# Causal attention and two feed-forward layers: odd heads' score halves swapped from the 13th pair on, and both decay products of those pairs on VectorE

## The chip, the cores and the metric

The kernel runs on one core of a Trainium2 chip. The metric is the device time of one execution in microseconds. TensorE (PE) multiplies matrices into PSUM, VectorE (DVE), ScalarE (ACT) and GpSimd (POOL) work element by element, and SyncE (SP) issues every DMA of this kernel, one after the other. Each engine runs its own list of instructions in order and waits for the others by semaphores.

## The reference, cut to what matters

```python
# attention: batch 4, heads 8, sequence 768, head_dim 48
for t in range(S):
    cur = einsum('bhd,bhe->bhde', u * k[t], v[t])
    y[t] = einsum('bhd,bhde->bhe', r[t], state + cur)
    state = w[t][..., None] * state + einsum('bhd,bhe->bhde', k[t], v[t])
# then, on (3072, 384) tokens:
xn = x / sqrt(mean(x * x) + 1e-6) * rms_g
x = (silu(xn @ w_gate) * (xn @ w_val)) @ w_out          # d_ff 1536
y = (s * relu(x @ w_in) ** 2 + b) @ w_out               # d_ff 2048
```

## The kernel before

The sequence is cut into 6 chunks of 128 tokens. A chunk of one batch row is a pair, numbered jb = 0 to 23 (chunk jb // 4, batch row jb % 4); the 13th pair is jb = 12. A pair's attention is worked as follows.

- DMAs bring w, then r and k together, then r and k by token (`n`), then v.
- VectorE scans the decays into `E` (line 357) and, backwards, into `bk` (line 364). Both are the tile `eb`, of which the later pairs have one copy, so the scan of the next pair waits until all readers of the last are done. r is multiplied by `E` and k by `bk`, in place in the tile `in` (`tt`, recorded at line 316); from jb = 12 on either engine, VectorE or GpSimd, may take each product, as the planner decides.
- `scores` (line 404): PE multiplies k by r. Two heads share a tile, one in partitions 0 to 47 and one in 64 to 111 (p = 0, 1, which write two PSUM banks); h = 0 to 3 counts the tiles. Only tokens of k not later than those of r count, so k's tokens 0 to 63 (c0 = 0) meet 128 columns of r, and tokens 64 to 127 (c0 = 64) only the last 64. The k half sits in columns c0 to c0 + 63 of PE's array and its result in the same partitions of PSUM. So each matmul uses a quarter of the array.
- ScalarE copies each score bank to a tile `a`, and GpSimd clears what lies above the diagonal (`affine_select`, line 426).
- `sums`: `state` (line 445) multiplies r by the state, line 454 multiplies `a` by v into the same banks, and `news` (line 463) multiplies the transposed k (`raw`, brought by four `kt` DMAs from `kd`) by v for the next state. VectorE adds `av` into `ys` and the news into `st`; the result is normalised and, from jb = 12 on, transposed through DRAM (`turn_x`: `pat`, then `xt` DMAs).

Meanwhile PE works through the first feed-forward layer, chunk after chunk, in steps f: `mm_in` for gate and for value (line 646, nine matmuls of 128x512 each, in banks 0 and 1), ScalarE's silu and VectorE's product (`sg`, which reads the value's bank), ScalarE's `hh` and VectorE's `hl`, and three `mm_out` of three matmuls each (lines 629 to 631) into banks 2, 3 and 4. After the last f of a chunk these banks are copied out (`o`, line 681 on ScalarE, 683 on VectorE) before the next chunk's first `mm_out` writes them.

Nothing of the order is written by hand. `op` hands each operation with a due time, a cost for each engine that may take it and what it reads and writes to `Plan`; `Plan.issue` plays the plan through with these costs and emits the instructions in the order in which that play starts them. A table, `FIRST_OPS`, replaces due times by operation number up to number 921; jb = 12 begins at operation 964. So a new operation or cost shifts the order of all engines after it.

Of the kernel before, what the change touches and what calls it, by code (L numbers as in the profile page):

```python
# [17 lines left out]
ALU = mybir.AluOpType  # L18
# [4 lines left out]
B, H, S, D = 4, 8, 768, 48  # L23
C = 128
NC = S // C
HP = H // 2
DM = H * D
# [20 lines left out]
W_TINY, W_HUGE = 1.125 * 2.0 ** -15, 1.875 * 2.0 ** 16 - 2.0 ** -7  # L48
FA, HALF = 6, (4, 6)
ATT = 30.0, 6.0, 0.0, 18.0, 20.0, 20.0, 20.0, 0.0  # L50
TD, LATE = 3, 60
ORDER = -200, -190, -170, -160, -180, -150
FIRST_OPS = {
# [170 lines left out]
def body(ctx: ExitStack, tc: tile.TileContext, rkw, nat, w1, w2, cst, out):  # L224
    nc = tc.nc
# [5 lines left out]
    def tiles(n, name, shape, dt=F32):  # L231
        return [sb.tile(shape, dt, name=f"{name}{i}") for i in range(n)]
# [15 lines left out]
    OT = tiles(2, "o", [128, NB])  # L248
    IN = tiles(2, "in", [128, RKW])
    VT = tiles(2, "v", [128, H, D])  # L250
    NT, = tiles(1, "n", [128, 2, H, D])
    EB = [[t] for t in tiles(2, "eb", [RW, HP, WL])]
    KT = tiles(1, "kt", [128, HP, RW])
# [48 lines left out]
    def op(when, engines, fn, reads=(), writes=(), port=True):  # L302
        if planned[0]:
            reads, writes = [alias.get(k, k) for k in reads], [alias.get(k, k) for k in writes]
            plan.add(when, engines, fn, reads, writes, port)
        else:
            fn(next(iter(engines)))

    def dma(when, dst, src, nbytes, reads=(), writes=(), land=0.0):
        op(when, {"sp": max(0.47, nbytes / 350e3 + 0.06) + 0.5 * (when == -300)}, lambda e: nc.sync.dma_start(  # L310
            out=dst, in_=src), reads, writes, land)
# [23 lines left out]
    def attention(jb, t):  # L335
        q, b = jb % 2, jb % B
        AVK = [("av", q, h0) for h0 in range(0, H, 2)]
        ke, re, ne = (DVE, DVE, DVE) if jb < EARLY else (BOTH, BOTH, BOTH)
        last = jb >= NJ - B
        a, v, g, z = IN[q][:RW], VT[q], RG[q], q if jb < NZ else 0  # L340
        n = [RK[z][:, i * DM:(i + 1) * DM].rearrange("p (h d) -> p h d", h=H) for i in range(2)]
        ET, BT, kt, xg = EB[0][z], EB[1][z], KT[z], XG[z]
        ek, bk, nk, tk, xk = ("E", z), ("bk", z), ("n", z), [("kt", z)], ("xg", z)
        turned = jb >= TURNED
        rk = RK[z][:RW, 0:HP * C].rearrange("p (h t) -> p h t", h=HP)
        r = a[:, OR:OK].rearrange("p (h t) -> p h t", h=HP)
        k = a[:, OK:].rearrange("p (h t) -> p h t", h=HP)
# [5 lines left out]
        if jb >= NU:  # L353
            dma(tl[2], RK[z], nat[jb, :, DM:], 128 * 2 * DM * 4, (), [nk])
        dma(tl[3], v.rearrange("p h d -> p (h d)"), nat[jb, :, 0:DM], 128 * DM * 4, (), [("v", q)])

        op(t, {"dve": 1.15}, lambda e: nc.vector.tensor_tensor_scan(
            ET.rearrange("p h t -> p (h t)"), a[:, 0:HP * WL], ones.rearrange("p h t -> p (h t)"), 0.0,
# [39 lines left out]
        def scores(e):  # L398
            for h in range(HP):
                for c0 in (0, 64) if jb >= B else (0,):  # L400
                    cols = slice(c0, c0 + 64 if jb >= B else C)
                    for p in range(2):
                        rows = slice(64 * p, 64 * p + D)
                        nc.tensor.matmul(sc[p][cols, h, c0:], k[rows, h, cols], r[rows, h, c0:],  # L404
                                         start=True, stop=True, skip_group_check=True)
            if kp is not None:
                for h in range(HP):
                    nc.tensor.transpose(kp[:, h, :], k[:, h, :], ident[:RW, :RW])  # L408
# [12 lines left out]
        for p in range(2):  # L421
            if jb < NM:
                tt(t, DVE, HP * C, AT[A[p]], sc[p], mask, ALU.mult, [("ps", i2[p]), "m"], [("a", A[p])])
                continue
            cp(t, HP * C, AT[A[p]], sc[p], [("ps", i2[p])], [("a", A[p])])
            op(t, {"pool": 0.60}, lambda e, s=A[p]: nc.gpsimd.affine_select(  # L426
                out=AT[s], in_=AT[s], compare_op=ALU.is_gt, fill=0.0, base=0, pattern=[[0, HP], [1, C]],
                channel_multiplier=-1), (), [("a", A[p])])
        if kp is not None:
            cp(t, HP * RW, kt, kp, [("ps", i)], tk)  # L430
        if jb < NU:
# [16 lines left out]
        def sums(e):  # L448
            if jb >= B:
                state(e)  # L450
            for j in range(H):
                h, p = divmod(j, 2)
                for c0 in (0, 64):
                    nc.tensor.matmul(Y[p][c0:c0 + 64, j, :], AT[A[p]][:, h, c0:c0 + 64], v[:, j, :],  # L454
                                     start=jb < B and j == 0, stop=j >= H - 2, skip_group_check=True)
            if U is not None and jb >= B:
                news(e)
# [19 lines left out]
        if jb < B:  # L477
            op(t, {"pe": 1.0}, sums, reads + [("v", q)], [("ps", i)])
            op(t, {"pe": 0.7}, more, AVK + ["cs"], [("ps", i)])
            op(t, {"pe": 0.6}, news, [("v", q)] + tk, [("ps", iu)])  # L480
            ys, yk = PS[i][:, 0:DM], ("ps", i)
        else:
            op(t, {"pe": 1.5 + 0.6 * (not last)}, sums,
               reads + [("r", q), ("v", q), ("st", b)] + tk * (not last),
               [("ps", i) for i in iy] + ([] if last else [("ps", iu)]))
            ys, yk = YS[q], ("ys", q)
            for p in range(2):
                y2, a2, s2 = [x.rearrange("p (h j d) -> p h j d", h=HP, j=2)[:, :, p] for x in (
                    PS[iy[p]][:, 0:DM], AV[q].rearrange("p h d -> p (h d)"), ys)]
                tt(t, DVE, HP * D, s2, y2, a2, ALU.add, [("ps", iy[p])] + AVK, [yk])  # L490
# [403 lines left out]
    for c in range(NC):  # L894
        t2 = T1 + c * d2
        x = c % 2
# [139 lines left out]
```

## Time and profile before

| | |
|---|---|
| time, median of 3 runs | 967.43 us (966.9 to 967.6) |
| the profiled execution | 967.64 us, of which its span is 965.9 us |
| PE busy | 952.9 us, 99% of the span |
| DVE, ACT, POOL busy | 635.2, 378.8 and 162.6 us |
| the chain that ended last | PE 91%, DVE 5%, DMA 2%, ACT 1% |

Busy time of PE is the time in which any of its pipelined matmuls was under way, so it says that PE was never without work, and not that it was at its peak. The profiled execution is one run; its time lies 0.2 us above the median.

### The profile page before, as it was taken

Reading aid. Unit: us, or ns where it says so; the run is one execution under the profiler, and the core shown is the slowest. Engines: PE = TensorE matmul, PEld = TensorE weight load, DVE = VectorE, ACT = ScalarE, POOL = GpSimd, SP = SyncE. Lnnn points to the kernel's source line nnn. Section 1 sums busy time; section 2 is a strip of 40 time slices with the busy share of each in tenths; the row PEclk is TensorE's granted clock in tenths of the full one; section 3 lists DMA queues with packets and bytes.
Section 4 is the critical chain, followed back from the end, with each engine's and each line's share of the span. In section 5 each row is a group of like instructions: output and inputs, shape, how many; then the busy total and the mean of one; then the engine's idle time right before and its main releaser. Section 6 shows DMA issues by size and latency. Waiting matters only on the chain.

```text
span 965.9 us, 16522 instructions
## 1 busy us (share of the span) xinstructions
PE 952.9 (99%) x6585; PEld 788.7 (82%) x6589; DVE 635.2 (66%) x1051; ACT 378.8 (39%) x782; POOL 162.6 (17%) x211
## 2 busy tenths in 40 slices
PE   9999999999999999999999999999999999999996
PEld 5898998888888887888888878888888888888885
DVE  8999898547445445532588799987777874433332
ACT  4756545534323332332343353343433433433333
POOL 1212211255433323110025440000000000000000
PEclk9999999999999999999999999999999999999998
DMA  8655554245434443222466465553354530000001
GB/s 259 196 169 158 173 158 140 83 112 149 101 84 118 122 93 95 69 69 61 122 225 206 150 212 178 158 194 113 114 182 132 178 117 1 33 0 1 34 1 36
DMA packets 74422, 115.79 MB, mean 120 GB/s; under 512 B 28384, under 2 KB 48096, under 8 KB 74336
## 3 DMA queue, kind: packets, MB, share of 16 engines
q1 hardware_dynamic: 74336, 114.65, 39.6%
q8 instruction: 53, 0.87, 0.4%
q14 instruction: 33, 0.27, 0.1%
HBM read 99.16 MB, written 15.47 MB: 119 GB/s over the span
## 4 chain that ended last, share of the span: by engine, by line
PE 91%; DVE 5%; DMA 2%; ACT 1%; issue 1%; SPq 0%; POOL 0%; DVEq 0%
PE b L646 48%; PE b L629 12%; PE b L630 11%; PE b L631 11%; PE b L454 2%; PE b L404 2%; PE b L445 1%; DMA raw<-in_w 1%; DMA in<-in_rkw 1%; DVE pat L605 1%; DVE pat L603 1%; PE b L408 0%; PE b L822 0%; PE b L469 0%; DVE pat L599 0%
## 5 line engine op out<-in xcount | busy, mean ns | idle before, releaser
L646 PE MATMUL b<-xh,w 128*128 128x512 f32 (+1 forms) x1566 | 485.2, 374 | 0.9 <-DVE sg L316 0.6
L646 PEld LDWEIGHTS b<-xh,w 128*128 128x128 f32 x1566 | 287.7, 188 | 55.6 <-issue 1.9
L646 PE MATMUL b<-xl,w 128*128 128x512 f32 (+1 forms) x783 | 291.1, 372 | 0.0
L629 PE MATMUL b<-hh,w 128*128 128x512 f32 (+1 forms) x537 | 205.0, 382 | 1.1 <-ACT in L681 0.7
L630 PE MATMUL b<-hl,w 128*128 128x512 f32 (+1 forms) x537 | 202.5, 377 | 1.4 <-DVE hl L316 1.4
L631 PE MATMUL b<-hh,w 128*128 128x512 f32 (+1 forms) x537 | 202.1, 376 | 0.0
L319 ACT ACTIVATE sg<-b 128x512 f32<-128x512 f32 (+1 forms) x179 | 102.6, 573 | 249.1 <-PE b L646 245.0
L646 PEld LDWEIGHTS b<-xl,w 128*128 128x128 f32 x783 | 147.3, 188 | 25.4
L717 DVE SCALAR_TENSOR_TENSOR sg<-sg,cs,b 128x512 f32<-128x512 f32 (+1 forms) x97 | 71.9, 741 | 90.0 <-ACT sg L319 89.8
L630 PEld LDWEIGHTS b<-hl,w 128*128 128x128 f32 x537 | 101.0, 188 | 20.2 <-DVE hl L316 2.5
L629 PEld LDWEIGHTS b<-hh,w 128*128 128x128 f32 x537 | 101.0, 188 | 20.1 <-ACT in L681 0.9
L631 PEld LDWEIGHTS b<-hh,w 128*128 128x128 f32 x537 | 101.0, 188 | 18.5
L720 DVE SCALAR_TENSOR_TENSOR hl<-sg,cs,hh 128x512 fp32r<-128x512 f32 (+1 forms) x97 | 73.0, 753 | 43.4 <-ACT hh L319 43.2
L319 ACT ACTIVATE hh<-sg,cs 128x512 fp32r<-128x512 f32 (+1 forms) x97 | 70.1, 722 | 75.9 <-DVE sg L717 71.4
L319 ACT ACTIVATE hh<-sg 128x512 fp32r<-128x512 f32 (+1 forms) x82 | 47.6, 581 | 114.9 <-DVE sg L316 109.5
L316 DVE TENSOR_TENSOR sg<-b,sg 128x512 f32<-128x512 f32 (+1 forms) x82 | 51.0, 623 | 62.1 <-PE b L646 52.9
L316 DVE TENSOR_TENSOR hl<-sg,hh 128x512 fp32r<-128x512 f32 (+1 forms) x82 | 57.3, 698 | 18.2 <-ACT hh L319 17.5
L620 POOL TENSOR_TENSOR w<-pat,w 128x384 fp32r<-128x384 f32 x29 | 39.8, 1394 | 67.2 <-ACT w L610 67.2
L610 ACT ACTIVATE w<-pat 128x384 fp32r<-128x384 f32 x68 | 32.8, 520 | 37.5 <-DVE pat L605 37.3
L316 DVE TENSOR_TENSOR ys<-b,av 128x192 f32<-128x192 f32 x40 | 13.8, 351 | 47.8 <-PE b L454 47.8
L426 POOL TENSOR_SCALAR_AFFINE_SELECT a<-a 128x512 f32<-128x512 f32 x38 | 29.6, 796 | 85.7 <-ACT a L319 85.4
L603 DVE SCALAR_TENSOR_TENSOR pat<-raw,pat 128x768 uint32<-128x768 uint32 (+1 forms) x40 | 35.7, 894 | 0.0
(128 smaller groups left out, 843.4 us busy)
## 6 DMA issues: line engine op xcount, KB each, us to landing
raw<-in_w SPq DMA_DIRECT2D x56, 768.0 KB, 4.4
in<-in_rkw SPq DMA_DIRECT2D x24, 448.0 KB, 4.6
raw<-in_w SPq DMA_DIRECT2D x24, 384.0 KB, 3.6
n<-in_nat SPq DMA_DIRECT2D x18, 384.0 KB, 3.4
in<-in_rkw SPq DMA_DIRECT2D x24, 226.6 KB, 3.0
x2d<-o SPq DMA_DIRECT2D x21, 256.0 KB, 2.4
a<-in_rkw SPq DMA_DIRECT2D x24, 224.0 KB, 2.9
v<-in_nat SPq DMA_DIRECT2D x24, 192.0 KB, 4.0
```

Of the source, the lines that this page charges most:

```text
L316: op(when, {e: cost[e] for e in engines}, lambda e: E[e].tensor_tensor(dst, a, b, f), reads, writes, port)
L319: op(when, {"act": act(n)}, lambda e: nc.scalar.activation(dst, src, func, **kw), reads, writes)
L426: op(t, {"pool": 0.60}, lambda e, s=A[p]: nc.gpsimd.affine_select(out=AT[s], in_=AT[s], compare_op=ALU.is_gt, fill=0.0, base=0, pattern=[[ ...
L603: op(t, {"dve": vec2(N)}, lambda e, word=word, pat=pat: nc.vector.scalar_tensor_tensor(pat(), word(1), 0xC0000000, pat(), ALU.bitwise_and, ...
L610: op(t, {"act": act(DM)}, lambda e, c=c, s=s, pat=pat: nc.scalar.activation(W[s][:, 0], pat(c).bitcast(F32), AF.Copy), [("pat", pi)], [("w ...
L620: op(t, {"dve": vec2(DM)} if ph == 0 else {"dve": vec2(DM), "pool": gps(DM)}, lambda e, c=c, s=s, pat=pat: E[e].tensor_tensor(W[s][:, 1], ...
L629: nc.tensor.matmul(dst, wt[:, 0, cols], xh, start=first, stop=False, skip_group_check=True)
L630: nc.tensor.matmul(dst, wt[:, 0, cols], xl, start=False, stop=False, skip_group_check=True)
L631: nc.tensor.matmul(dst, wt[:, 1, cols], xh, start=False, stop=last, skip_group_check=True)
L646: nc.tensor.matmul(dst, W[s][:, w, kk * 128:(kk + 1) * 128], xx[x][:, kk, sl], start=first and j == kk == 0, stop=last and kk == KD - 1 an ...
L717: op(t, {"dve": vec2(n)}, lambda e: nc.vector.scalar_tensor_tensor(sg, sg, s_col, p, ALU.mult, ALU.mult), [("ps", i)], [("sg", q)], False)
L720: op(t, {"dve": vec2(n)}, lambda e: nc.vector.scalar_tensor_tensor(hl, sg, b_col, hh.bitcast(F32), ALU.add, ALU.subtract), [("sg", q), ("h ...
```

## The change

For jb of 12 and up (`EVEN`), the scores of odd h go to the other half of the array's columns: k's tokens 0 to 63 to columns and partitions 64 to 127, and tokens 64 to 127 to 0 to 63. The rows of `a` of these heads are then swapped, so `sums` multiplies them by a copy of v with swapped token halves, `VS`, which two more DMAs per pair bring (each 64 tokens, the odd tiles' heads). One select per tile becomes three: even h as before, and the two halves of odd h with their own diagonals. And both decay products (`ke`, `re`) are given to VectorE alone.

```diff
--- before.py
+++ after.py
@@ -48,7 +48,7 @@
 W_TINY, W_HUGE = 1.125 * 2.0 ** -15, 1.875 * 2.0 ** 16 - 2.0 ** -7
 FA, HALF = 6, (4, 6)
 ATT = 30.0, 6.0, 0.0, 18.0, 20.0, 20.0, 20.0, 0.0
-TD, LATE = 3, 60
+TD, LATE, EVEN = 3, 60, 12
 ORDER = -200, -190, -170, -160, -180, -150
 FIRST_OPS = {
     0: 281.6, 22: 529.2, 37: 729.3, 38: 985.1, 39: 488.5, 46: 298.9, 57: 804.2, 58: 733.2, 64: 673.4, 75: -711.3,
@@ -248,6 +248,7 @@
     OT = tiles(2, "o", [128, NB])
     IN = tiles(2, "in", [128, RKW])
     VT = tiles(2, "v", [128, H, D])
+    VS = tiles(2, "vs", [128, HP, D])
     NT, = tiles(1, "n", [128, 2, H, D])
     EB = [[t] for t in tiles(2, "eb", [RW, HP, WL])]
     KT = tiles(1, "kt", [128, HP, RW])
@@ -335,13 +336,13 @@
     def attention(jb, t):
         q, b = jb % 2, jb % B
         AVK = [("av", q, h0) for h0 in range(0, H, 2)]
-        ke, re, ne = (DVE, DVE, DVE) if jb < EARLY else (BOTH, BOTH, BOTH)
+        ke, re, ne = (DVE, DVE, DVE) if jb < EARLY else (DVE, DVE, BOTH)
         last = jb >= NJ - B
         a, v, g, z = IN[q][:RW], VT[q], RG[q], q if jb < NZ else 0
         n = [RK[z][:, i * DM:(i + 1) * DM].rearrange("p (h d) -> p h d", h=H) for i in range(2)]
         ET, BT, kt, xg = EB[0][z], EB[1][z], KT[z], XG[z]
         ek, bk, nk, tk, xk = ("E", z), ("bk", z), ("n", z), [("kt", z)], ("xg", z)
-        turned = jb >= TURNED
+        turned, even = jb >= TURNED, jb >= EVEN
         rk = RK[z][:RW, 0:HP * C].rearrange("p (h t) -> p h t", h=HP)
         r = a[:, OR:OK].rearrange("p (h t) -> p h t", h=HP)
         k = a[:, OK:].rearrange("p (h t) -> p h t", h=HP)
@@ -353,6 +354,11 @@
         if jb >= NU:
             dma(tl[2], RK[z], nat[jb, :, DM:], 128 * 2 * DM * 4, (), [nk])
         dma(tl[3], v.rearrange("p h d -> p (h d)"), nat[jb, :, 0:DM], 128 * DM * 4, (), [("v", q)])
+        if even:
+            for z in (0, 64):
+                dma(tl[3], VS[q][z:z + 64].rearrange("p (g x) d -> p g (x d)", g=2),
+                    nat[jb, 64 - z:128 - z, 0:DM].rearrange("t (g o m) -> t g o m", g=2, o=2)[:, :, 1],
+                    64 * 4 * D * 4, (), [("vs", q, z)])
 
         op(t, {"dve": 1.15}, lambda e: nc.vector.tensor_tensor_scan(
             ET.rearrange("p h t -> p (h t)"), a[:, 0:HP * WL], ones.rearrange("p h t -> p (h t)"), 0.0,
@@ -399,9 +405,10 @@
             for h in range(HP):
                 for c0 in (0, 64) if jb >= B else (0,):
                     cols = slice(c0, c0 + 64 if jb >= B else C)
+                    to = slice(64 - c0, C - c0) if even and h % 2 else cols
                     for p in range(2):
                         rows = slice(64 * p, 64 * p + D)
-                        nc.tensor.matmul(sc[p][cols, h, c0:], k[rows, h, cols], r[rows, h, c0:],
+                        nc.tensor.matmul(sc[p][to, h, c0:], k[rows, h, cols], r[rows, h, c0:],
                                          start=True, stop=True, skip_group_check=True)
             if kp is not None:
                 for h in range(HP):
@@ -423,9 +430,18 @@
                 tt(t, DVE, HP * C, AT[A[p]], sc[p], mask, ALU.mult, [("ps", i2[p]), "m"], [("a", A[p])])
                 continue
             cp(t, HP * C, AT[A[p]], sc[p], [("ps", i2[p])], [("a", A[p])])
-            op(t, {"pool": 0.60}, lambda e, s=A[p]: nc.gpsimd.affine_select(
-                out=AT[s], in_=AT[s], compare_op=ALU.is_gt, fill=0.0, base=0, pattern=[[0, HP], [1, C]],
-                channel_multiplier=-1), (), [("a", A[p])])
+            def keep(t, what, cost, base, n):
+                op(t, {"pool": cost}, lambda e, what=what: nc.gpsimd.affine_select(
+                    out=what, in_=what, compare_op=ALU.is_gt, fill=0.0, base=base, pattern=[[0, n], [1, what.shape[-1]]],
+                    channel_multiplier=-1), (), [("a", A[p])])
+
+            if not even:
+                keep(t, AT[A[p]], 0.60, 0, HP)
+                continue
+            pairs = AT[A[p]].rearrange("p (g o) t -> p g o t", o=2)
+            keep(t, pairs[:, :, 0], 0.37, 0, 2)
+            keep(t, pairs[0:64, :, 1], 0.37, -64, 2)
+            keep(t, pairs[64:128, :, 1, 0:64], 0.25, 0, 2)
         if kp is not None:
             cp(t, HP * RW, kt, kp, [("ps", i)], tk)
         if jb < NU:
@@ -451,7 +467,8 @@
             for j in range(H):
                 h, p = divmod(j, 2)
                 for c0 in (0, 64):
-                    nc.tensor.matmul(Y[p][c0:c0 + 64, j, :], AT[A[p]][:, h, c0:c0 + 64], v[:, j, :],
+                    vj = VS[q][:, j // 4 * 2 + p] if even and h % 2 else v[:, j, :]
+                    nc.tensor.matmul(Y[p][c0:c0 + 64, j, :], AT[A[p]][:, h, c0:c0 + 64], vj,
                                      start=jb < B and j == 0, stop=j >= H - 2, skip_group_check=True)
             if U is not None and jb >= B:
                 news(e)
@@ -481,7 +498,7 @@
             ys, yk = PS[i][:, 0:DM], ("ps", i)
         else:
             op(t, {"pe": 1.5 + 0.6 * (not last)}, sums,
-               reads + [("r", q), ("v", q), ("st", b)] + tk * (not last),
+               reads + [("r", q), ("v", q), ("st", b)] + [("vs", q, z) for z in (0, 64)] * (jb >= EVEN - 2) + tk * (not last),
                [("ps", i) for i in iy] + ([] if last else [("ps", iu)]))
             ys, yk = YS[q], ("ys", q)
             for p in range(2):
```

The order of the instructions changes from jb = 11 on. Here are three places. First PE at `sums` of jb = 16 (bank 0 is `b_156` before and `b_158` in the change, the banks count up from there; line 445 before is 461 in the change, 629 to 631 are 646 to 648, 646 is 663). Before:

```order
L646 MATMUL b_156<-xh_116,w_1588 128x512
L629 MATMUL b_158<-hh_122,w_1589 128x512
L630 MATMUL b_158<-hl_124,w_1589 128x512
L631 MATMUL b_158<-hh_122,w_1589 128x512
L445 MATMUL b_161<-st_71,in_128 64x48
...
L463 MATMUL b_163<-v_130,raw_111 64x48 x8
L629 MATMUL b_159<-hh_122,w_1589 128x512
...
L629 MATMUL b_160<-hh_122,w_1589 128x512
...
L646 MATMUL b_157<-xh_116,w_1587 128x512
```

In the change:

```order
L663 MATMUL b_158<-xh_116,w_1590 128x512
L646 MATMUL b_160<-hh_122,w_1591 128x512
...
L646 MATMUL b_161<-hh_122,w_1591 128x512
...
L646 MATMUL b_162<-hh_122,w_1591 128x512
L647 MATMUL b_162<-hl_124,w_1591 128x512
L648 MATMUL b_162<-hh_122,w_1591 128x512
L461 MATMUL b_163<-st_71,in_128 64x48
...
L480 MATMUL b_165<-v_130,raw_111 64x48 x8
L663 MATMUL b_159<-xh_116,w_1589 128x512
```

`sums` stood behind the first of the three `mm_out` and now stands behind all three.

Second VectorE from the `hl` ahead of the decay products of jb = 18 (`in_128`) on; `eb_133` and `eb_134` are `E` and `bk` before, `eb_135` and `eb_136` in the change, `o_127<-b_160` (`b_162` in the change) is the copy out of bank 4. Before:

```order
L316 TENSOR_TENSOR hl_125<-sg_121,hh_123 128x512
L316 TENSOR_TENSOR in_128<-in_128,eb_134 112x512
L316 TENSOR_TENSOR sg_120<-b_157,sg_120 128x512
L510 STREAM_TRANSPOSE raw_111<-in_128 128x4x4x32
L357 SCALAR_TENSOR_TENSOR eb_133<-in_129,ones_68 112x516
L316 TENSOR_TENSOR hl_124<-sg_120,hh_122 128x512
L362 RECIPROCAL rg_70<-eb_133 112x4x8
L390 TENSOR_REDUCE ac_146<-n_132 128x8
L683 COPY o_127<-b_160 128x512
```

In the change:

```order
L317 TENSOR_TENSOR hl_125<-sg_121,hh_123 128x512
L317 TENSOR_TENSOR in_128<-in_128,eb_135 112x512
L317 TENSOR_TENSOR in_128<-in_128,eb_136 112x512
L317 TENSOR_TENSOR sg_120<-b_159,sg_120 128x512
L527 STREAM_TRANSPOSE raw_111<-in_128 128x4x4x32
L317 TENSOR_TENSOR hl_124<-sg_120,hh_122 128x512
L363 SCALAR_TENSOR_TENSOR eb_135<-in_129,ones_68 112x516
L396 TENSOR_REDUCE ac_148<-n_134 128x8
L368 RECIPROCAL rg_70<-eb_135 112x4x8
L700 COPY o_127<-b_162 128x512
```

The product of r has come in ahead of that of k, `hl` has moved ahead of the scan of the next pair, and the copy still stands behind both.

Third SP around the r,k load of jb = 14 (`in_128`, 112x1024). Before:

```order
L310 DMA kd_166<-raw_111 32x4x128 x4
L310 DMA in_128<-in_rkw 112x1024
L310 DMA raw_111<-kd_166 128x4x32 x4
L310 DMA v_130<-in_nat 128x384
L310 DMA in_128<-in_rkw 112x518
L310 DMA n_132<-in_nat 128x768
L310 DMA xt_168<-pat_113 32x4x96 x4
```

In the change:

```order
L311 DMA kd_168<-raw_111 32x4x128 x4
L311 DMA n_134<-in_nat 128x768
L311 DMA in_128<-in_rkw 112x518
L311 DMA raw_111<-kd_168 128x4x32 x4
L311 DMA in_128<-in_rkw 112x1024
L311 DMA v_130<-in_nat 128x384
L311 DMA x2d_172<-o_126 128x512
L311 DMA x2d_172<-o_127 128x512
L311 DMA vs_132<-in_nat 64x2x96 x2
L311 DMA xt_170<-pat_113 32x4x96 x4
```

The load stood ahead of the four `kt` loads of jb = 13 (`raw<-kd`) and now stands behind them; the two `VS` loads stand behind `v`.

## Rows read from the trace of the kernel before

**Rows 1.** The page: the span, busy time of PE, the chain.

```profile
span 965.9 us, 16522 instructions
...
PE 952.9 (99%) x6585; PEld 788.7 (82%) x6589; DVE 635.2 (66%) x1051; ACT 378.8 (39%) x782; POOL 162.6 (17%) x211
...
PE 91%; DVE 5%; DMA 2%; ACT 1%; issue 1%; SPq 0%; POOL 0%; DVEq 0%
```

**Rows 2.** Busy time by stretch: from:to, length, engines (instructions), granted clock, DMA.

```profile
240.00:480.00 240.00, 239.60 (x2056) 194.52 (x2056) 108.99 (x169) 75.67 (x145) 61.33 (x85) 1.00 0.37 94
```

**Rows 3.** Timeline of PE, scores of jb = 19: start, us, instruction.

```profile
373.64 1.10 PE L404 MATMUL b<-in 48*64 48x128 f32 x32
374.67 0.50 PE L646 MATMUL b<-xh,w 128*128 128x512 f32 x1
```

**Rows 4.** Line 404 in the stretch 373.60 to 373.70.

```profile
L404 PEld LDWEIGHTS b<-in x5: 129/129/133, 373.6 to 373.7; 48*64 48x64 f32 x5
L404 PE MATMUL b<-in x4: 267/294/320, 373.6 to 373.7; 48*64 48x128 f32 x2, 48*64 48x64 f32 x2
```

**Rows 5.** Timeline of PE, `sums` of jb = 16 and what follows.

```profile
310.84 0.68 PE L445 MATMUL b<-st,in 48*64 48x48 f32 x32
...
312.99 0.50 PE L629 MATMUL b<-hh,w 128*128 128x512 f32 x1
```

**Rows 6.** Timeline of SP after it.

```profile
313.08 2.53 SPq L310 DMA_DIRECT2D raw<-kd  x4
315.65 0.50 SPq L310 DMA_DIRECT2D in<-in_rkw  x1
316.20 0.43 SPq L310 DMA_DIRECT2D v<-in_nat  x1
```

**Rows 7.** Timeline of VectorE after it: last, idle before and its releaser.

```profile
320.38 0.69 DVE L316 TENSOR_TENSOR in<-in,eb 112x512 f32<-112x512 f32 x1 [1.56 <-DMA in<-in_rkw]
320.99 0.69 DVE L316 TENSOR_TENSOR sg<-b,sg 128x512 f32<-128x512 f32 x1
...
322.22 1.79 DVE L357 TENSOR_TENSOR_SCAN eb<-in,ones 112x516 f32<-112x516 f32 x1
...
325.19 0.67 DVE L683 COPY o<-b 128x512 f32<-128x512 f32 x1
325.78 1.22 DVE L364 TENSOR_TENSOR_SCAN eb<-in,rg 112x516 f32<-112x516 f32 x1
```

**Rows 8.** Timeline of PE there, first `mm_out` of chunk 3.

```profile
324.70 0.39 PE L629 MATMUL b<-hh,w 128*128 128x512 f32 x1
...
326.07 0.40 PE L629 MATMUL b<-hh,w 128*128 128x512 f32 x1
```

**Rows 9.** Timeline of GpSimd, selects: the constant mask, and jb = 18.

```profile
2.02 0.29 POOL L817 TENSOR_SCALAR_AFFINE_SELECT mk<-mk 128x128 f32<-128x128 f32 x1
...
353.03 1.25 POOL L426 TENSOR_SCALAR_AFFINE_SELECT a<-a 128x512 f32<-128x512 f32 x2 [0.42 <-ACT a L319]
```

**Rows 10.** Timeline of PE, where `sums` first reads them.

```profile
355.53 1.14 PE L454 MATMUL b<-v,a 128*64 128x48 f32 x32
```

**Rows 11.** Timeline of PE around its wait near 369 us.

```profile
368.78 0.39 PE L629 MATMUL b<-hh,w 128*128 128x512 f32 x1
369.56 0.50 PE L630 MATMUL b<-hl,w 128*128 128x512 f32 x1 [0.40 <-DVE hl L316]
```

**Rows 12.** Timeline of VectorE, product of k of jb = 16 and the next `hl`.

```profile
276.69 0.69 DVE L316 TENSOR_TENSOR in<-in,eb 112x512 f32<-112x512 f32 x1 [1.88 <-DMA in<-in_rkw]
...
278.68 1.09 DVE L316 TENSOR_TENSOR hl<-sg,hh 128x512 fp32r<-128x512 f32 x1
```

**Rows 13.** Timeline of PE where it reads that `hl`.

```profile
280.90 0.39 PE L630 MATMUL b<-hl,w 128*128 128x512 f32 x1
```

**Rows 14.** Timeline of PE, after `sums` of jb = 12, and first `mm_out` of chunk 2.

```profile
226.29 0.50 PE L629 MATMUL b<-hh,w 128*128 128x512 f32 x1
...
238.69 0.39 PE L629 MATMUL b<-hh,w 128*128 128x512 f32 x1
```

## Prediction

> **What bounds the kernel.** I read the page first: TensorE is busy 952.9 of 965.9 us and the chain that ended last is 91% PE [rows 1]. So an edit pays only if it makes PE's own list shorter, and costs only where it makes PE wait. The change touches pairs jb = 12 to 23, whose work lies between 198 and 480 us, so I then read that stretch: from 240 to 480 us PE is busy 239.60 of 240.00 us [rows 2], and its only idle there is the 0.40 us at 369.56, a wait for VectorE's `hl` [rows 11]. VectorE is busy 109.0 of those 240 us and GpSimd 61.3 [rows 2]. Neither is a bound by its sum; what matters is whether VectorE, which runs its list in order, stands still on one late input while the next PE input is behind it. So I read, around each pair, the PE, VectorE and SP rows in order of time.
>
> **The scores: the gain.** The 32 score records of a pair occupy PE from 373.64 until the next line starts at 374.67, 1.03 us [rows 3]. A pair has 4 heads x 2 column halves x 2 row halves, each in two passes. All four quarters run at once: within the first 0.1 us, four matmuls of both widths have begun [rows 4]. A quarter then works alone through its list. The quarter of columns 0 to 63 has 8 passes of 128 columns. PE passes 512 columns in 0.227 us (324.70 to 326.07 is six such matmuls) [rows 8], so 128 columns are 0.057 us; 8 passes at that rate would be 0.45 us and at twice that 0.91, and the block is 1.03 with its start, so a pass costs 0.114 us. After the change every quarter has 4 passes of 128 and 4 of 64 columns: 4 x 0.114 + 4 x 0.057 = 0.68 us. Gain 0.22 us a pair, 12 pairs: **-2.6 us**. Bounds: 0.26 a pair if the whole 1.03 us scales with the longest list (-3.1), nothing if issue order or weight loads keep the quarters from running ahead (0). I take 0.22, because the block's length already follows the longest quarter. The products with `v` keep their number and size; half read `VS`.
>
> A rule speaks against this gain. The Trainium skill ("TensorE: Matmul & The Clock Gate", section on packing small matmuls) says that a weight load overlaps running matmuls only if it is for other rows of the array; by it the two column halves of one row half would not overlap, and balancing them would give 0 in place of -2.6. Rows 4 disagree: five weight loads are under way beside four matmuls within 0.1 us, and there are only two row halves.
>
> **The masks.** One 128x512 select per tile becomes three: 128x256, 64x256, 64x128. The trace has 0.29 us for 128x128 and 1.25 for two of 128x512 [rows 9], so on a line 0.40, 0.40 and 0.29, 2.2 us per pair instead of 1.25. Bounds: 1.25 x 640/512 = 1.6 (by columns alone, which are 256 + 256 + 128) and 6 x 0.63 = 3.8 (size costs nothing). For jb = 18 the selects start at 353.03 and `sums` first reads them at 355.53 [rows 9, 10]. The planner has moved `sums` behind more `mm_out` (0.68 us each), so the need is at 355.53 + 0.68 - 0.22 = 356.0 and 353.03 + 2.2 = 355.2 is in time: 0. If the cover is gone (3.8 us), PE waits 0.8 us.
>
> **The order that follows.** Later `sums` release the next pair's loads later. `sums` of jb = 16 runs from 310.84 to 312.99 [rows 5]; then SP issues four `kt` loads (313.08) and the r,k load of jb = 18 (315.65) [rows 6], which lands at 320.38, where VectorE has idled 1.56 us for it [rows 7]: 7.4 us after `sums`. With two `mm_out` put before `sums` it lands at 320.38 + 1.36 = 321.74. And VectorE now has the r product (0.61 us, start to start as k's in rows 7) ahead of everything behind k.
> - jb = 18: the copy `o<-b` out of bank 4 stands 4.81 us behind k [rows 7], and PE writes that bank again at 326.07 [rows 8], 0.2 us after the copy ended. Now it stands behind the landing by 4.81 + 0.61 for r, less 0.57 because the scan took 1.79 beside GpSimd's product and 1.22 is the undisturbed one [rows 7], plus some 0.2 for `hl`, which now waits for ScalarE: 321.74 + 5.05 = 326.8, over at 327.45. PE waits 1.4 us and loses 0.11 at the restart (the first matmul after a wait takes 0.50, any other 0.39) [rows 8, 11]: **+1.5**.
> - jb = 16: `hl` starts 1.99 us behind k [rows 12], so at 276.69 + 1.36 + 0.61 + 1.99 = 280.65, over at 281.3; PE needs it at 280.90 [rows 13]: **+0.5**.
> - jb = 14: r and k were GpSimd's. Now r stands on VectorE ahead of `sg`, and SP issues its load only after the four `kt`. `sums` of jb = 12 ended at 226.29 [rows 14]; with three `mm_out` put before it and a shorter score block it ends at 226.29 + 2.04 - 0.22 = 228.1. The load lands 6.9 us later (four `kt`, the issue and 4.7 us, as in rows 6 and 7 without the slow `kt`), then come r (0.61), a transpose (0.6) and `sg` (0.69): 236.9. PE wants the bank that `sg` reads 2.04 us before 238.69 [rows 14], less 0.22: 236.4. With the restart **+0.6**.
> - jb = 15: likewise. `sums` of jb = 13 stands behind two `mm_out` and one `val` more, the load lands 6.9 us after it, and r, k and `sg` take 1.91: 8.8 us after `sums`. PE wants the bank after `gate`, `mm_out`, `val` and `gate`, 4 x 2.04 + 0.11 = 8.3 us after `sums`: **+0.6**.
> - jb = 20: PE already lost 0.55 + 0.11 us here [rows 11]. The order puts `val` before this `mm_out`, which gives 2 us, and takes it back by r, the scan, `g`, `ac` and the second scan ahead of `hl`. About 0.5 is left (`sg`, 3.1 us behind the landing at 365.30 + 0.68, holds the bank until 369.1, wanted at 368.78; `hl` is 0.1 late after it): **-0.15**.
> - jb = 17, 19, 21 to 23: slack of 0.4 us or more stays: 0.
> - GpSimd's `av` now runs beside r and k. The scan's 1.79 against 1.22 [rows 7] prices such a meeting at 0 to 0.6 us; I take 0.1 at four of the places: **+0.4**. The Trainium skill ("SBUF — State Buffer", section on the two sides) calls the port of VectorE and GpSimd an exclusive lock; the trace agrees (1.79 against 1.22), and by it the term could be the whole of `av` at each place.
> - SP: two `VS` DMAs a pair, some 0.43 us each like the `v` issue [rows 6], behind r,k and `v`, so the r,k landing doesn't move; their use is some 15 us later: 0.
>
> Sum: -2.6 + 1.5 + 0.5 + 0.6 + 0.6 - 0.15 + 0.4 = **+0.85 us**. Against the profiled execution (967.64 us with its span of 965.9) that is 968.5; its time is 0.2 above the median of 967.43, so I say **968.3 us**. Later waits (0.65 us near 557) hang on transfers that PE itself releases, so a shift passes through.
>
> **Rivals.** 0.2% of this time, 1.9 us, is about what a measurement of this kernel can tell from none.
> - The stalls eat the gain (forecast), 966.6 to 969.3: 0.47.
> - The gain comes through. The stalls of jb = 14 to 18 all rest on the r,k load landing later by what `sums` moved. If the load's 7.4 us shrink, or `sg` and `hl` have more slack than I worked out, they go, the old 0.66 goes too, and 967.4 - 2.6 - 0.5 = 964.3 is left. For it: half of the time VectorE is free. Against it: it idled for that load in rows 7 and 12 already. 0.2.
> - Slower, selects at a fixed cost of 0.63: PE waits 0.8 us in the seven pairs where `sums` moved by one `mm_out`: 968.3 + 5.6 = 973.9. It decides from some 0.5 us per select up. Rows 9 speak against it (0.29 for the small one). 0.1.
> - The swap doesn't shorten the scores (the column halves don't run ahead of one another): 968.3 + 2.6 = 970.9. Rows 4 speak against it. 0.08.
> - GpSimd's `av` costs VectorE the 0.57 us of rows 7 at each of the five places named: 968.3 - 0.4 + 2.85 = 970.8. 0.15.
> Faster 0.2, same 0.47, slower 0.33. The range reaches from near the second case to the last two, and leaves out the dear selects and the lower half of the second: 964.9 to 971.0.
>
> **What would show it.** The score block about 0.8 us in place of 1.03. Selects of 0.40, 0.40, 0.29. PE idle of about 1.4 us just before the third `mm_out` group of the first f of chunk 3 (near 326), released by VectorE's `o<-b`; smaller ones for `sg` or `hl` near 236, 259 and 281. VectorE's idle before r in place of before k. If PE has no new idle there, the load landed earlier than I say and the kernel is faster; if it waits at `sums` for GpSimd, the selects are dearer.

## The result: slower by 0.67%

The changed kernel takes 974.14 us (median of 5 runs, 971.51 to 979.70), beside 967.60 us for the kernel before on the same chip (5 runs, 966.90 to 967.85): a ratio of 1.0067 [1.0043, 1.0092]. Measured once more, later, it was 973.50 us against 967.50, 1.0055 [1.0036, 1.0074]. The forecast was 968.3 us, in a range up to 971.0.

The profiled execution is the longest of the five, 979.70 us with a span of 978.0. Part of that isn't the change's. The first rows answer to [rows 1], the next to [rows 2]; the 16 us from 8 us on stand with them, of after and then of before. In the page and the tables `mm_in` is L663 here, `mm_out` L646 to L648, the scores L411, the products with `v` L471, VectorE's two-operand helper L317. Page of the changed kernel:

```profile
span 978.0 us, 16623 instructions
...
PE 958.8 (98%) x6585; PEld 791.7 (81%) x6589; DVE 645.7 (66%) x1072; ACT 376.2 (38%) x780; POOL 145.9 (15%) x240
...
PE 86%; DVE 7%; DMA 3%; SPq 2%; issue 1%; ACT 1%; DVEq 0%; ACTq 0%
```

Busy time by stretch, changed kernel (PE, PEld, VectorE, ScalarE, GpSimd; then the granted clock, the DMA share and GB/s):

```profile
8.00:24.00 16.00, 14.96 (x133) 11.40 (x136) 13.07 (x22) 6.02 (x22) 1.36 (x5) 0.68 0.71 216
...
240.00:480.00 240.00, 233.96 (x2023) 188.03 (x2022) 115.00 (x180) 71.70 (x137) 56.03 (x117) 0.99 0.36 92
290.00:294.00 4.00, 4.00 (x11) 3.18 (x12) 2.99 (x4) 0.00 (x0) 0.15 (x1) 0.58 0.62 155
```

The same view of the kernel before, its start alone:

```profile
8.00:24.00 16.00, 15.36 (x179) 11.16 (x182) 16.00 (x27) 9.36 (x34) 2.18 (x5) 1.00 0.91 283
```

Two things are to be seen. From 8 to 24 us, where both kernels run the same program, TensorE had a granted clock of 0.68 instead of 1.00; by the scores of jb = 4 the changed kernel was 4.7 us late, and the scores of jb = 12, where the change begins, start 5.0 us later than before. The kernel before with one planner figure altered for the late pairs alone (below) was 4.75 us late by jb = 12 in its profile, at 0.68 as well. So this is a difference between executions, and I leave it out of the comparison. From there to jb = 23, shifts of the score blocks tell the rest: they go from +5.0 to +12.7 us. The stretch of the change lost 7.7 us, where I had forecast +0.85 for it.

From 240 to 480 us PE is now busy 233.96 us in place of 239.60 [rows 2]. Whom it waited for is in the table of waits, from 230 to 400 us (engine, line, releaser: us in total, times, longest); before, the only wait was one of 0.4 us, for `hl` [rows 11]:

```profile
PE b L663 <- DVE sg L317: 2.4, 3, 1.1
PE b L646 <- ACT hh L320: 2.2, 2, 1.3
PE b L646 <- DVE o L700: 1.0, 1, 1.0
PE b L647 <- DVE hl L317: 0.4, 2, 0.2
```

All of them lead to VectorE: `sg` and `o<-b` are its own, and `hh` and `hl` follow from `sg`. The scores did get shorter: 0.84 us from start to the next line in place of 1.03 [rows 3].

```profile
387.16 0.90 PE L411 MATMUL b<-in 48*64 48x128 f32 x32
388.00 0.50 PE L663 MATMUL b<-xh,w 128*128 128x512 f32 x1
```

How long VectorE waits for the r,k load, 250 to 400 us (in total, times, longest), first in the kernel before, then in the changed one:

```profile
DVE in L316 <- DMA in<-in_rkw: 9.6, 6, 2.4
```

```profile
DVE in L317 <- DMA in<-in_rkw: 16.6, 6, 4.0
```

In six pairs VectorE stands 16.6 us in front of the r,k load, 7.0 more than before, with `sg`, `hl` and `o<-b` behind. The pair jb = 16 shows it. VectorE's timeline (it answers to [rows 7, 12]):

```profile
285.99 1.93 DVE L317 TENSOR_TENSOR in<-in,eb 112x512 f32<-112x512 f32 x2 [4.03 <-DMA in<-in_rkw]
287.85 0.68 DVE L317 TENSOR_TENSOR sg<-b,sg 128x512 f32<-128x512 f32 x1
...
289.22 0.69 DVE L317 TENSOR_TENSOR hl<-sg,hh 128x512 fp32r<-128x512 f32 x1
```

GpSimd's, at the same time:

```profile
286.38 0.99 POOL L317 TENSOR_TENSOR av<-v,ac 128x384 f32<-128x384 f32 x1 [6.53 <-DMA v<-in_nat]
```

And PE's:

```profile
287.55 0.39 PE L663 MATMUL b<-xh,w 128*128 128x512 f32 x1
289.24 0.50 PE L646 MATMUL b<-hh,w 128*128 128x512 f32 x1 [1.31 <-ACT hh L320]
289.97 0.50 PE L647 MATMUL b<-hl,w 128*128 128x512 f32 x1 [0.22 <-DVE hl L317]
...
291.27 0.63 PE L648 MATMUL b<-hh,w 128*128 128x512 f32 x1
291.69 0.63 PE L646 MATMUL b<-hh,w 128*128 128x512 f32 x1
```

The two products take 1.93 us together, where they take 1.29 if nothing comes between them (last section): GpSimd's `av` begins 0.39 us behind the landing, when its `v` has come, and stands between r and k. So `sg` comes late, `hh` and then `hl` with it, and PE waits twice. Then seven 512-column matmuls run at the lower of the clock's two levels, 1.2 GHz (0.43 us from start to start, as at 291.27, where 0.227 is usual). That costs another 1.4 us, and shows as the 0.58 of the stretch 290 to 294 us above.

### The profile page after: what moved, and what is told of

Same layout as the page of the kernel before. It is cut to its first block, busy times and chain, and to the rows that moved or that the text cites. A ratio compares the mean times of both kernels' runs of the same rounds, so it can differ in the third digit from the quotient of the medians.

```text
span 978.0 us, 16623 instructions
## 1 busy us (share of the span) xinstructions
PE 958.8 (98%) x6585; PEld 791.7 (81%) x6589; DVE 645.7 (66%) x1072; ACT 376.2 (38%) x780; POOL 145.9 (15%) x240
## 4 chain that ended last, share of the span: by engine, by line
PE 86%; DVE 7%; DMA 3%; SPq 2%; issue 1%; ACT 1%; DVEq 0%; ACTq 0%
PE b L663 45%; PE b L646 11%; PE b L647 11%; PE b L648 11%; PE b L471 2%; PE b L411 2%; DMA in<-in_rkw 2%; SPq L311 2%; PE b L461 1%; DVE in L317 1%; DVE pat L622 1%; DVE pat L620 1%; DVE sg L317 1%; PE b L839 1%; DVE w L637 1%
## 5 line engine op out<-in xcount | busy, mean ns | idle before, releaser
L663 PE MATMUL b<-xh,w 128*128 128x512 f32 (+1 forms) x1566 | 487.1, 375 | 3.0 <-DVE sg L317 2.6
L663 PEld LDWEIGHTS b<-xh,w 128*128 128x128 f32 x1566 | 288.3, 189 | 58.2 <-DVE sg L317 4.6
L663 PE MATMUL b<-xl,w 128*128 128x512 f32 (+1 forms) x783 | 291.7, 373 | 0.0
L646 PE MATMUL b<-hh,w 128*128 128x512 f32 (+1 forms) x537 | 205.3, 382 | 3.9 <-ACT hh L320 2.2
L648 PE MATMUL b<-hh,w 128*128 128x512 f32 (+1 forms) x537 | 202.7, 377 | 0.0
L663 PEld LDWEIGHTS b<-xl,w 128*128 128x128 f32 x783 | 147.5, 189 | 25.1
L646 PEld LDWEIGHTS b<-hh,w 128*128 128x128 f32 x537 | 101.2, 188 | 24.1 <-ACT hh L320 3.0
L648 PEld LDWEIGHTS b<-hh,w 128*128 128x128 f32 x537 | 101.3, 189 | 18.2
L317 DVE TENSOR_TENSOR sg<-b,sg 128x512 f32<-128x512 f32 (+1 forms) x82 | 50.6, 617 | 64.8 <-PE b L663 50.8
L317 DVE TENSOR_TENSOR hl<-sg,hh 128x512 fp32r<-128x512 f32 (+1 forms) x82 | 55.2, 673 | 15.9 <-ACT hh L320 14.8
L434 POOL TENSOR_SCALAR_AFFINE_SELECT a<-a 128x256 f32<-128x256 f32 (+3 forms) x86 | 39.1, 476 | 80.3 <-ACT a L320 78.7
L317 DVE TENSOR_TENSOR in<-in,eb 112x512 f32<-112x512 f32 x40 | 32.3, 828 | 23.8 <-DMA in<-in_rkw 23.7
L317 DVE TENSOR_TENSOR ys<-b,av 128x192 f32<-128x192 f32 x40 | 13.7, 349 | 45.2 <-PE b L471 45.2
```

Source lines behind the costliest of these rows:

```text
L317: op(when, {e: cost[e] for e in engines}, lambda e: E[e].tensor_tensor(dst, a, b, f), reads, writes, port)
L434: op(t, {"pool": cost}, lambda e, what=what: nc.gpsimd.affine_select(out=what, in_=what, compare_op=ALU.is_gt, fill=0.0, base=base, patter ...
L646: nc.tensor.matmul(dst, wt[:, 0, cols], xh, start=first, stop=False, skip_group_check=True)
L648: nc.tensor.matmul(dst, wt[:, 1, cols], xh, start=False, stop=last, skip_group_check=True)
L663: nc.tensor.matmul(dst, W[s][:, w, kk * 128:(kk + 1) * 128], xx[x][:, kk, sl], start=first and j == kk == 0, stop=last and kk == KD - 1 an ...
```

## Experiments

Each kernel was timed in 5 rounds (6 to 12 executions) beside the kernel before on its chip. Medians of before were 968.07 us for the first four, 967.44 for the next four, 967.50 for the last four. The theories have the names of the expectations. A: VectorE's products behind a late landing hold `sg`, `hl` and the store copy; A1 says that their place in the order costs, A2 that their own length does, stretched beside `av`. B: the swap's own DMAs and selects. C: `sums`, put later by the planner.

**The swap alone.**

```diff
-        ke, re, ne = (DVE, DVE, DVE) if jb < EARLY else (DVE, DVE, BOTH)
+        ke, re, ne = (DVE, DVE, DVE) if jb < EARLY else (BOTH, BOTH, BOTH)
```

> The swap alone: the r and k products are again left to the planner for both engines, as before. Theory A (VectorE's r product, done late beside GpSimd's av, holds sg, hl and the store copy): the stalls of pairs 14, 15 and 16 shrink or go and 32 scores in 0.89 us instead of 1.10 bring 12 x 0.21 = 2.5 us: 965 to 968 us. Theory B (the swap's own DMAs and selects make the wait): the time stays near the changed kernel, 972 to 974 us. Theory C (sums put later by the planner, whatever VectorE does): about half of the loss stays, 969 to 971 us.

969.93 us, 1.0018 [1.0003, 1.0034]. Less than half of the loss is left, so the two products on VectorE, with the order that they bring, make the larger part. The number itself lies in C's range and above A's. The planner puts `sums` later here as well, and PE waits for `sg` of jb = 14 (1.75 us over the usual 0.227) and for `hl` of jb = 20 (0.84).

**The products alone.**

```diff
-TD, LATE, EVEN = 3, 60, 12
+TD, LATE, EVEN = 3, 60, 99
```

> Both products on VectorE from pair 12 on, no swap, no VS loads, one select per tile. Theory A: the stalls stay, without the gain: 970 to 974 us. Theory B: as before, 967 to 968 us. Theory C: sums stand almost where they stood before, so one or two of the stalls are left: 968 to 970 us.

972.07 us, 1.0039 [1.0026, 1.0051]: in A's range. More than half of the loss is there without a swap, its DMAs or its selects, so B alone can't be it. The profile shows waits for `hl`, `o<-b` and `sg` at jb = 18 and 20 alone, and its score blocks fall back by 2.5 us from jb = 12 to 23; the rest of the 3.8 us isn't seen in it. `sums` stand one or two `mm_out` later at jb = 13 to 16 and 18 here too, so C isn't out yet.

**The swap alone, in the old order.** The planner is told 0.60 for the first select of a tile, 0 for the two others and 0 for the `VS` loads.

```diff
 (on top of the swap alone)
-            keep(t, pairs[:, :, 0], 0.37, 0, 2)
-            keep(t, pairs[0:64, :, 1], 0.37, -64, 2)
-            keep(t, pairs[64:128, :, 1, 0:64], 0.25, 0, 2)
+            keep(t, pairs[:, :, 0], 0.60, 0, 2)
+            keep(t, pairs[0:64, :, 1], 0.0, -64, 2)
+            keep(t, pairs[64:128, :, 1, 0:64], 0.0, 0, 2)
-                dma(tl[3], VS[q][z:z + 64]...)
+                op(tl[3], {"sp": 0.0}, ... the same dma_start ...)
```

> The swap alone, and the planner is told the old costs (0.60 for the first select of a tile, 0 for the other two, 0 for the VS loads), so that sums and VectorE's list stand from pair 15 on as before. What the swap itself does to the chip's time is all that differs. Theories A and C: 964.5 to 966 us (967.5 less 2.5, the old wait at pair 20 kept). Theory B: 970 us or more, TensorE waiting at sums for the selects or for VS.

966.57 us, 0.9988 [0.9976, 1.0001]. That is a little above the range of A and C, and B falls for the swap by itself: with its selects and its DMAs in place there is no loss, and PE waits for neither from 230 to 400 us. The gain that I had worked out is there in part: the score blocks move 1.13 us forward between jb = 12 and 23, where 11 x 0.21 = 2.3 were to be had; the old wait of jb = 20 is still there (0.48), new ones of 0.32 us near 252 and 0.24 near 325 take from it, and the rest is in smaller gaps.

**Both parts, with the old costs.** The same edit on the changed kernel.

> Both parts of the change, but with the old planner costs for selects and VS loads, so that sums stand where they stood before. Theory A: the r product stays in VectorE's way; 968 to 972 us. Theory C: the stalls of pairs 14 to 18 go and the gain comes through; 964.5 to 966.5 us. Theory B: 972 to 975 us.

973.75 us, 1.0067 [1.0048, 1.0085]. The loss stays, though `sums` of jb = 14 and 15 stand where they stood before the change. That speaks against C, but doesn't settle it: the number lies in B's range and above A's, and the table of waits has one for the selects that the changed kernel doesn't have:

```profile
PE b L664 <- DVE sg L317: 2.8, 2, 2.1
PE b L472 <- POOL a L435: 1.7, 4, 0.5
PE b L648 <- DVE hl L317: 0.9, 3, 0.4
```

PE now waits at `sums` for the selects, four times, 1.7 us in all. The planner's later `sums` in the changed kernel are what hides the selects; without them PE pays directly.

**The late landing told to the planner.** The planner takes a load to land 2.0 us after its issue; this adds 2.7 for the r,k load.

```diff
-        dma(tl[1], a[:, OR:], rkw[jb, :, OR:], RW * 2 * HP * C * 4, (), [("r", q), ("k", q)])
+        dma(tl[1], a[:, OR:], rkw[jb, :, OR:], RW * 2 * HP * C * 4, (), [("r", q), ("k", q)], 2.7 * (jb >= EVEN))
```

> The whole change, and the planner is told that the r,k load lands 2.7 us later than it assumes (4.7 us after its issue, as traced), so it puts sg, hl and the store copy ahead of r and k where they would be ready first. Theory A1 (the order on VectorE against the landing is what costs): the stalls of pairs 14 to 18 shrink to a few tenths, 966 to 969 us beside 968 of before. Theory A2 (the products' own time, stretched beside GpSimd's av, costs wherever they stand): 971 to 974 us. Theory B (DMAs of the swap): 973 to 975 us.

966.44 us, 0.9987 [0.9972, 1.0003]. All of the loss goes, with both products on VectorE, the same selects and the same DMAs. And `sums` of jb = 13 to 15 still stand one or two `mm_out` later than before the change, so their place by itself doesn't make the loss: C falls here. VectorE's timeline at jb = 16 (the place of 285.99 above):

```profile
277.49 0.69 DVE L317 TENSOR_TENSOR sg<-b,sg 128x512 f32<-128x512 f32 x1 [2.00 <-PE b L663]
279.60 0.55 DVE L396 TENSOR_REDUCE ac<-n 128x8 f32<-128x384 f32 x1 [1.42 <-POOL av L317]
280.07 0.68 DVE L317 TENSOR_TENSOR in<-in,eb 112x512 f32<-112x512 f32 x1
280.67 0.68 DVE L317 TENSOR_TENSOR hl<-sg,hh 128x512 fp32r<-128x512 f32 x1
281.27 0.69 DVE L317 TENSOR_TENSOR in<-in,eb 112x512 f32<-112x512 f32 x1
```

`sg` is done before the products, `hl` stands between them, and no product waits for its load any more (the row `in <- DMA in<-in_rkw` is gone from VectorE's waits). The new order also puts `ac`, a sum that VectorE makes from `n`, ahead of them, and in the trace it waits for `av` (1.42 us). So `av` is over, at 279.56 us, when the first product starts, and the two don't meet, at jb = 16 or at any pair from 15 to 20: this run takes away the early place of the products and the stretch at once, and can't tell one from the other. What PE still waits for from 230 to 400 us is one line:

```profile
PE b L663 <- DVE sg L317: 1.1, 2, 0.8
```

**A short `av`.** The order stays that of the changed kernel, instruction by instruction.

```diff
-                tt(td, BOTH, DM, AV[q], v, AC[q].to_broadcast([128, H, D]), ALU.mult,
-                   [("ac", q), ("v", q)], AVK)
+                w = 1 if jb >= EVEN else H
+                op(td, {"dve": vec2(DM), "pool": gps(DM)}, lambda e: E[e].tensor_tensor(
+                    AV[q][:, 0:w], v[:, 0:w], AC[q][:, 0:w].to_broadcast([128, w, D]), ALU.mult),
+                   [("ac", q), ("v", q)], AVK)
```

> The whole change in its own order, but GpSimd's av product takes one head of eight in pairs 12 to 23 (leaves out seven eighths of that product, so the current-token term of those heads is stale); nothing else moves. Theory A2: r and k take 1.2 us instead of 1.9 and the stalls of pairs 14, 15, 16, 18 and 20 lose 0.6 us each or go: 3 us or more faster than the changed kernel, 969 to 971.5 us. Theory A1: at most 0.1 to 0.3 us a stall, 973 to 974.5 us.

970.41 us, 1.0028 [1.0016, 1.0039]: 0.39% less than the changed kernel had at first and 0.27% less than at the second measurement, 2.6 to 3.8 us. VectorE and GpSimd at jb = 16:

```profile
279.55 1.37 DVE L317 TENSOR_TENSOR in<-in,eb 112x512 f32<-112x512 f32 x2 [3.02 <-DMA in<-in_rkw]
280.84 0.68 DVE L317 TENSOR_TENSOR sg<-b,sg 128x512 f32<-128x512 f32 x1
...
280.09 0.28 POOL L402 TENSOR_TENSOR av<-v,ac 128x48 f32<-128x48 f32 x1 [5.66 <-DMA v<-in_nat]
```

The products take 1.37 us in place of 1.93, and PE's waits from 230 to 400 us come to 2.4 us in place of 6.0. So A2's stretch is real, and makes some half of the loss. What the order costs without it is the 2.7 us that are left here (1.0028). No run has the better order of the late landing with the stretch left in.

**Without the `VS` loads.**

```diff
-                dma(tl[3], VS[q][z:z + 64]...)
+                op(tl[3], {"sp": 0.47}, lambda e: None, (), [("vs", q, z)], 0.0)
-                    vj = VS[q][:, j // 4 * 2 + p] if even and h % 2 else v[:, j, :]
+                    vj = v[:, j, :]
```

> The whole change in its own order without the two VS loads of a pair; odd heads of pairs 12 to 23 multiply by V as it lies (leaves out the turned copy of V, so these heads come out wrong). Theory B (the two DMAs push kt and the r,k load back): 970 us or less, the r,k load landing sooner after sums. Theories A1 and A2: 973.5 to 975 us, as the changed kernel.

972.90 us, 1.0052 [1.0034, 1.0070]. This lies between the two ranges. The interval takes in both measurements of the changed kernel, so no more than a part of the loss can be the loads'; PE still waits for VectorE at six pairs, five of them those of the changed kernel, and once for a select (0.6 us). What they add (by the ratios 0.3 to 1.5 us, within the intervals nothing) stays open.

**The swap alone, with the old costs and the late landing.** Both edits above on the swap alone.

> The swap alone with the old costs and, besides, the late landing told to the planner. Theory A1: the half microsecond left at hl of pair 20 and the 0.3 near 252 us go too: 964 to 966 us, a little under the swap alone in the old order. If the order matters little: 966.5 us as that one.

968.22 us, 1.0004 [0.9988, 1.0019]: a miss. PE has a new wait of 2.1 us at 239.8 us, behind which the granted clock is 0.50 from 243.7 to 247 us (some 1.3 us more), and one of 0.9 at 328. The better figure isn't a gain in itself; each new figure gives another order, and with it other small waits. By such shuffling the time moved 1.5 us here (from 0.9988); the loss that goes with the late landing told is over four times that.

**The kernel before, with the late landing.**

```diff
-        dma(tl[1], a[:, OR:], rkw[jb, :, OR:], RW * 2 * HP * C * 4, (), [("r", q), ("k", q)])
+        dma(tl[1], a[:, OR:], rkw[jb, :, OR:], RW * 2 * HP * C * 4, (), [("r", q), ("k", q)], 2.7 * (jb >= 12))
```

> The kernel before, with only the planner's estimate of the r,k landing raised by 2.7 us for pairs 12 to 23. If the late landing told is a gain by itself, as much as the whole change lost: 963 to 966 us. If it only mends what the change did to VectorE's list (theory A1): 967 to 968.5 us, the wait at pair 20 (0.66 us) perhaps gone and another come.

966.91 us, 0.9996 [0.9982, 1.0010]: no change that can be told. The figure mends what the change did; it isn't a gain that was lying there. This is the kernel whose profile ran at 0.68 from 8 to 24 us:

```profile
8.00:24.00 16.00, 14.57 (x131) 11.05 (x133) 12.88 (x20) 5.55 (x21) 1.46 (x5) 0.68 0.69 207
```

**The products alone, with the late landing.** `EVEN` 99 and `2.7 * (jb >= 12)`.

> Both products on VectorE, no swap, the late landing told to the planner. Theory A1 says that the products cost nothing once sg, hl and the store copy stand ahead of them: 967 to 969 us in place of 972 for the products alone. Theory A2 (the time of the products themselves): 970.5 to 972.5 us.

969.15 us, 1.0012 [1.0001, 1.0023]: just above A1's range. Of the 3.8 us that the products alone cost, 2.6 go; waits for `hl` of 0.9 us near 281 and 0.6 near 371 stay.

**Both parts, the late landing and the old costs.**

> The whole change, the late landing told, and the old costs for the selects and the VS loads, so that sums stand as before the change. If the 1.0 us that the late landing alone left near 310 us comes from sums standing later: 964.5 to 966 us. If not: 966 to 968 us.

968.17 us, 0.9999 [0.9984, 1.0014], just above both ranges. Not better than the late landing alone, so nothing shows that the later `sums` were what that one lacked; PE waits for VectorE in other places here (0.4 to 0.7 us near 240, 282, 326 and 371).

**The changed kernel once more.**

> The changed kernel once more, on the same chip and against the same runs of before as the three others. Theories A1 and A2: 973 to 975 us, with r and k taking 1.9 us together where av starts 0.3 to 0.6 us after the landing, and the stalls at the same five places. Where the first 24 us run at the full granted clock (2.4 GHz), the span is 4 to 5 us shorter than in the first profile, which had the lower level there.

973.50 us, 1.0055 [1.0036, 1.0074]. In this second profile (977.58 us, again 0.68 from 8 to 24 us, so nothing is learned of a full clock there) PE waits 5.2 us from 230 to 400 us:

```profile
PE b L663 <- DVE sg L317: 3.3, 3, 1.3
PE b L646 <- DVE o L700: 1.0, 1, 1.0
PE b L646 <- ACT hh L320: 0.7, 1, 0.7
PE b L647 <- DVE hl L317: 0.2, 1, 0.2
```

The same five pairs, in other sizes: jb = 16 cost 1.5 us here, with no stretch at the lower clock behind it, and jb = 20 cost 1.2. The score blocks from jb = 12 to 23 lost 4.9 us, beside 7.7 in the first profile.

## Why the prediction was wrong

**Right: the scores.** 0.84 us a block in place of 1.03, a gain of 0.19 to 0.21 a pair where the sum had 0.22. The rule of the Trainium skill ("TensorE: Matmul & The Clock Gate", section on packing small matmuls), by which balancing the column halves would give nothing, doesn't agree with this measurement.

**Right: the selects.** From 300 to 480 us GpSimd's take 0.45, 0.40 and 0.29 us by shape (forecast 0.40, 0.40, 0.29), and PE doesn't wait for them in either profile of the changed kernel. The cover was thinner than I took it to be: with `sums` in their old places it is gone (1.7 us over four pairs).

**Right: the places.** The waits came at the five pairs named, jb = 14, 15, 16, 18 and 20, for the things named: `sg` at the first two, `hl` (and `hh` ahead of it) at 16, `o<-b` at 18, `sg` at 20. The rest of the list passed with nothing above 0.2 us.

**Wrong: their sizes.** This is the step that failed. Each figure is the time from the start of the last matmul ahead of a wait to the start of the next one, less the usual 0.227 us, with the 0.11 of the restart:

- jb = 14: forecast 0.6, measured 1.3 and 1.6 (the two profiles).
- jb = 15: forecast 0.6, measured 1.3 and 1.4.
- jb = 16: forecast 0.5, measured 2.1 and 1.5, and 1.4 for the lower clock in the first.
- jb = 18: forecast 1.5, measured 2.9 and 1.2.
- jb = 20: forecast 0.5, measured 0.6 and 1.2.

Together 3.7 was forecast, or 4.1 with the 0.4 for `av`, and 9.6 and 6.8 measured. With the scores (11 x 0.21 = 2.3 from jb = 12 to 23) and the old wait of 0.66, that explains 6.6 of the 7.7 us and 3.9 of the 4.9; the rest is in gaps under 0.3 us that I didn't follow up. Two terms of the sum carry the error.

The first is the port. I took 0.1 us at four places, and had 0.57 at five as a rival with a chance of 0.15. The runs show 0.64 (1.93 against 1.29) at four of the five in the first profile and at three in the second: the landing of r and k, which starts the products, is followed within 0.3 to 0.6 us by that of `v`, which starts `av`. Before, GpSimd did r itself in that time, and `av` came 1.7 us behind the landing, when VectorE's k was done. The change took away what kept them apart. I had written that `av` "now runs beside r and k" and priced it as a chance meeting. The Trainium skill ("SBUF — State Buffer", section on the two sides) has the port that the two engines share as an exclusive lock: the first holds it for a whole instruction, and the other stands still. The trace agrees in that the first wins (last section); the price is 0.64 us at whatever moment `av` begins up to 0.57 us behind the first product, not the 0.99 of its row.

The second is the landing. I took the r,k load to land 6.9 us after `sums` at jb = 14; it was 7.7 and 8.0 (the first from 233.19, where PE goes on behind `sums`, to 240.93, VectorE's first product):

```profile
233.19 0.50 PE L663 MATMUL b<-xh,w 128*128 128x512 f32 x1
240.93 0.69 DVE L317 TENSOR_TENSOR in<-in,eb 112x512 f32<-112x512 f32 x1 [3.29 <-DMA in<-in_rkw]
```

At jb = 16 it landed 8.6 and 8.0 us after them, where the trace of before, from which I took the term, has 7.7 (268.96 to 276.69), and at jb = 18 8.1 and 7.4 beside 7.4. SP's rows ahead of the load of jb = 18 in the first profile (they answer to [rows 6]), and VectorE's where it lands:

```profile
325.13 3.16 SPq L311 DMA_DIRECT2D raw<-kd  x4
328.35 0.49 SPq L311 DMA_DIRECT2D in<-in_rkw  x1
328.88 0.43 SPq L311 DMA_DIRECT2D v<-in_nat  x1
333.15 1.95 DVE L317 TENSOR_TENSOR in<-in,eb 112x512 f32<-112x512 f32 x2 [3.58 <-DMA in<-in_rkw]
```

The four `kt` issues took 3.16 us in place of 2.53, which is most of the 0.7 us there. It varies between executions, and the VectorE that stood before the load passed all of it on. At jb = 14, where `av` stretched nothing, the landing is the whole error.

Two things had no term at these pairs. A late `sg` delays `hh`, and `hl`, which is made of both, comes some 0.7 us behind `hh`; PE reads one after the other and waits for each, at jb = 16 in both profiles and at jb = 18 in the first (0.5 us each time for `hl`, beside 0.9 to 1.5 for `hh`). And the lower clock behind jb = 16 took 1.4 us of the first profile.

The rival that comes nearest to 974.14 by its number, the dear selects with 973.9, is wrong in its mechanism: PE never waits for a select in either profile of the changed kernel. (It counts seven pairs whose `sums` moved by one `mm_out`; the order has eight, jb = 15 and 17 to 23.) The nearest by mechanism is that of `av`, 970.8: it had the meeting, and not the later landings.

**What is shown and what isn't.** Shown: neither part of the change by itself makes the whole loss. In the old order the swap costs nothing, and the products in the planner's order cost 3.8 us. The loss hangs on the order that the planner made on a landing 2.7 us too early: with that one figure altered, the same work takes 966.44 us in place of 974. The meeting with `av` is 2.6 to 3.8 us of it, by the run with the short `av`. Open: whether the better order would give all of it back with the meeting left in, why the lower clock follows the two waits of jb = 16 in one profile and not in the other, and what the `VS` loads add.

Neither kernel that comes out under the one before (966.44 and 966.57 us) is proven faster: both intervals reach 1.

## What to carry to other kernels

On an engine that runs its list in order, an instruction moved behind a late load costs what it holds up behind it. So look first at what the mover does to the list, and ask whether the figure for that load's landing, by which a planner orders the list, is the traced one: here 2.7 us in one figure decided between 974 and 966 us. When work leaves an engine, look at what that engine does in the time instead; GpSimd's next product moved up to where the two engines meet.

## What was unexpected of the hardware

Whether the meeting costs anything turned on a few hundredths of a microsecond. Of 30 pairs (jb = 15 to 20 in five profiles with both products on VectorE and a whole `av` behind their landing), `av` began 0.57 us or less behind the first product in 23, and the two products took 1.93 to 1.95 us; in the seven others it began 0.59 us or more behind it, and they took 1.29 or 1.30. The second product starts 0.6 us behind the first, so by then it was ahead of `av`. Then it is `av` that is held up: its row is 1.28 to 1.39 us in the seven, and 0.83 to 1.01 in the 23. One of the seven is jb = 18 in the second profile of the changed kernel (VectorE, then GpSimd):

```profile
330.20 1.29 DVE L317 TENSOR_TENSOR in<-in,eb 112x512 f32<-112x512 f32 x2 [2.83 <-DMA in<-in_rkw]
330.82 1.36 POOL L317 TENSOR_TENSOR av<-v,ac 128x384 f32<-128x384 f32 x1 [5.57 <-DMA v<-in_nat]
```

After the waits of 1.31 and 0.22 us at jb = 16 the granted clock fell to the lower level for seven matmuls, a cost nearly as large as the waits (1.4 us); after waits of 0.88, 0.23 and 0.98 us at jb = 18 it didn't. The length of the wait alone doesn't decide it: the clock fell after one of 1.97 us in the swap alone with the old costs and the late landing, and not after one of 2.10 us in both parts with the old costs.
